# Re-placing weight preparation, weight fetches, a layer norm and down products in the feed-forward half of a transformer block

## The chip, the cores and the metric

The kernel runs on one core of a Trainium2 chip. A core has a matrix engine (TensorE, PE in the profile, with its weight loads as PEld), a vector engine (VectorE, DVE), a scalar engine (ScalarE, ACT), GpSimd (POOL) and SyncE (SP), which here only issues DMA transfers. Each engine runs its own queue of instructions in order and waits on semaphores for the others. The metric is the time of one execution in microseconds (us) on the device; lower is better.

## The reference

Input x is 2048 tokens of width 512. A conditioning vector c gives six rows of 512 (shift, scale and gate for each half). The block is an attention half and a feed-forward half, each on a layer norm:

```
h = layernorm(x) * (1 + ca) + sa
x = x + ga * attention(h)          # 32 heads, 4 segments of 512 tokens, local softmax plus a memory
h = layernorm(x) * (1 + cb) + sb
x = x + gb * (((h @ w_gate) * (h @ w_up)) @ w_down)     # hidden width 1376
```

All in float32. The change touches only the feed-forward half: layer norm, products with w_gate and w_up (512 x 1376), their elementwise product, and the product with w_down (1376 x 512) that is added to x.

## The kernel before

**Precision.** Each float32 operand is split into a high half (rounded, a copy on ScalarE) and a low half (operand minus high half, a subtraction on VectorE). A product is then three TensorE products: high x high, low x high, high x low (helper `six`, L1269, does this for two k-tiles of 128, so it issues six products).

**Feed-forward work.** The hidden width is eleven tiles f of 128 (the last, LAST = 10, is 96 wide). The four segments of 512 tokens are taken in two passes: pass p has segments 2p and 2p + 1 (index c). In a pass, pairs of tiles (i, i + 1) are computed by a scheme that gets the four blocks (two tiles x two segments) of a product with seven block products instead of eight. For this the inputs (`build`, L1223) and the weights (`wprep`, L459) are combined by additions into seven operands each, and each operand is split into halves. One such group of seven is a *unit* (`unit`, L1373): first "g" (gate), then "u" (up) for each pair. `units` (L394) is their list: n = 0 to 7 are the pairs 2, 4, 6, 8 of pass 0, n = 8 is "x" (tile LAST of pass 1, computed plainly by `open0`, `close0`, `other`), n = 9 to 18 are the pairs 2, 4, 6, 8, 0 of pass 1. Tiles 0, 1 and LAST of pass 0 are computed plainly ahead of unit 0 (L1497 to L1545).

**Inside a unit.** `unit` is a generator with six steps (its yields are numbered 1 to 6). The products go to the accumulators Z, Y, X, Y, X in turn; `out_of` copies an accumulator out on ScalarE (p5, p1, y), `add` (L1363) combines on VectorE, `finish` (L1349) multiplies gate and up (L1360) and `split` (L1289) makes the halves mH, mL of the result. The last two of the seven products, `seven` and `four`, run inside the next unit, ahead of its steps 2 and 4 (`prev(0)`, `prev(1)`). After `four` of a "u" unit, eight down products (`down`, L1323: two segments x four token tiles) go into the queue `dq`; `d()` pops one. A popped down product is 6 products into an accumulator (bank "acc"), an addition to the residual tile xa on VectorE (L1335), and for the last pair of a pass the store to the output. In pass 0 that store is followed at once by the load of the same xa buffer for pass 1 (`xload2`, L1321).

**Weights.** In pass 0, `wprep` loads raw weights, makes four sums on VectorE (tile cs), four high halves on ScalarE (cwH, L479) and four low halves on VectorE (cwL, L482). There are three buffers for prepared weights, used in turn. They are also stored to memory (`keep`). In pass 1 they are fetched back instead (`fetch`, L408: two transfers, then four copies on ScalarE, L416, in place). `wdprep` (L1297) does the same for w_down: in pass 0 load, multiply by the gate row gb (L1309), high half (L1310), low half (L1312); in pass 1 fetch and copy. `prepare(n)` joins them for unit n, as a generator of small steps.

**Order.** The Python program is unrolled by a planner that orders each engine's queue by a simulated time: an instruction that the planner believes ready may be placed ahead of instructions that stand earlier in the program. All TensorE products are chained in program order. `pin(i)` (L79) ties an instruction to the last product written before it, so that the planner cannot place it before that product; it adds no semaphore. The main loop (L1555) drives unit n, and at each step runs one step of `prepare(n + 2)` (two if unit n + 2 is a "u"), steps of other generators, and pops down products at the steps listed in `DS` (L1547):

```
DS = {"g": (1, 5, 6), "u": (1, 2, 4, 5, 6), "x": (1, 2, 4)}
if 1 <= n < CH - 1:
    next(lg, None)
```

`lg` is the layer norm of segments 2 and 3 (`lnC`, L568: loads; statistics L579, L580; scale factors; normalization L602; transposes on TensorE; L611). What of `prepare` is not done when unit n ends is run at once (`run(pr)`).

Of the kernel before, what the change touches and what calls it, by code (L numbers as in the profile page):

```python
# [8 lines left out]
F32 = mybir.dt.float32  # L9
F32R = mybir.dt.float32r  # L10
BF = mybir.dt.bfloat16
AF = mybir.ActivationFunctionType
# [6 lines left out]
S, D, H, DH, NSEG, L, F = 2048, 512, 32, 16, 4, 512, 1376  # L19
# [38 lines left out]
def tile_kernel(ctx, tc, x, wq, wk_, wv, wo, beta, w_gate, w_up, w_down, c, w_mod, out):  # L58
# [32 lines left out]
    vec, act = Switch(nc.vector), Switch(nc.scalar)  # L91
# [12 lines left out]
    btag = ["ms", "tb", "ms", "sm"]  # L104
# [49 lines left out]
    gbb = cst.tile([P, D], F32, name="gbb")  # L154
# [12 lines left out]
    def rows(s, t):  # L167
        return slice(s * L + t * P, s * L + (t + 1) * P)
# [224 lines left out]
    LAST = NF - 1  # L393
    units = [(0, nm, i) for i in range(2, LAST, 2) for nm in "gu"]  # L394
    CH = len(units)
    units += [(1, "x", LAST)] + [(1, nm, i) for i in (2, 4, 6, 8, 0) for nm in "gu"]
    NU = len(units)
    ENDS = (8, 0)
    wslot, plain = {}, {}
    wkeep, dkeep = {}, {}  # L400
# [7 lines left out]
    def fetch(key, tiles, store):  # L408
        for a, d in zip(tiles, store[key]):
            pin(nc.sync.dma_start(a.bitcast(F32), d))  # L410
        yield
        n = tiles[0].shape[1]
        for a in tiles:
            for i in range(0, n, 1024):
                b = a[:, i:min(n, i + 1024)]
                act.activation(b, b.bitcast(F32), AF.Copy)  # L416
                yield

    def xprep(n, tag, pool, rpool):
# [39 lines left out]
    def wprep(n, tag, pool, rpool):  # L459

        _, nm, i = units[n]
        if (nm, i) not in wkeep:
            raw = rpool.tile([P, KT, 2, P], F32, tag=f"raw{(n + 1) % 2}", name=f"cr{n}", bufs=1)
        wh = pool.tile([P, 7, 2, P], F32R, tag=f"wh{tag}", name=f"cwH{n}", bufs=1)
        wl = pool.tile([P, 7, 2, P], F32R, tag=f"wl{tag}", name=f"cwL{n}", bufs=1)
        wslot[n] = wh, wl
        if (nm, i) in wkeep:
            yield from fetch((nm, i), [a.rearrange("p a b c -> p (a b c)") for a in (wh, wl)], wkeep)
            return
        views = [w.rearrange("(k p) f -> p k f", p=P)[:, :, i * P:] for w in (w_gate, w_up)]  # L470
        pin(nc.sync.dma_start(raw.rearrange("p k r c -> p k (r c)"), views["gu".index(nm)][:, :, 0:2 * P]))
        yield
        S = rpool.tile([P, 4, 2, P], F32, tag="ws0", name=f"cs{n}", bufs=1)

        def A(r, c):
            return raw[:, 2 * c:2 * c + 2, r]

        def hi(d, v):
            act.activation(wh[:, d], v, AF.Copy)  # L479

        def lo(d, v):
            vec.tensor_sub(wl[:, d], v, wh[:, d].bitcast(F32))  # L482

        top = slice(4, 6), raw[:, :, 0].rearrange("p (c k) f -> p c k f", c=2)
        low = 6, A(1, 1)
        s1, s2 = ((d, S[:, d]) for d in (slice(0, 2), slice(2, 4)))
        vec.tensor_add(S[:, 0], A(1, 0), A(1, 1))
        vec.tensor_sub(S[:, 1], S[:, 0], A(0, 0))
        hi(*top)
        yield  # L490
        vec.tensor_sub(S[:, 2], A(0, 0), A(1, 0))
        vec.tensor_sub(S[:, 3], A(0, 1), S[:, 1])
        hi(*low)
        hi(*s1)
        yield
        lo(*top)
        hi(*s2)
        yield
        lo(*low)
        lo(*s1)  # L500
        yield
        lo(*s2)
        yield
# [641 lines left out]
    for v in range(-2, NQ + 1):  # L1145
        rate[0] = 5.5
        on, prev = 0 <= v < NQ, 0 <= v - 1 < NQ
        for slot in range(5):
            i = (slot + 3) % 5
            u = v + 2 if i < 3 else v + 1  # L1150
# [42 lines left out]
                    load(v + 3)  # L1193
            if slot == 1 and 3 <= v + 3 < NQ:
                until((v + 3) // 8, (v + 3) // 2 % 4)
    btag[:] = ["ms", "tb", "ms", "lk"]
    ps3 = [bank(f"wops3_{t}", shape=(P, 512)) for t in range(4)]
    for t in range(4):
        run(wo_row(ps3[t], t, us3, range(NG - 1)))
# [83 lines left out]
    def dbank(name):  # L1283
        nd[0] += 1
        return pst((P, 512), ("lq0", "lk0", "lq1", "lk1")[nd[0] % 4], name)
# [11 lines left out]
    def wdprep(p, f, tiles=None):  # L1297
        f0, n = ft[f]
        hi, lo = tiles or [bc.tile([P, D], F32R, tag="wd", name=f"d{x}{p}_{f}", bufs=8) for x in "HL"]
        wds[p, f] = hi, lo  # L1300
        if p > 0:
            yield from fetch(("d", f), (hi, lo), dkeep)
            return
        r = tmp(f"crd{p}_{f}") if tiles else wpool.tile([P, D], F32, tag="wor", name=f"crd{p}_{f}", bufs=2)
        pin(nc.sync.dma_start(r[0:n], w_down[f0:f0 + n, :]))
        if n < P:
            nc.gpsimd.memset(r[n:], 0.0)
        yield
        vec.tensor_mul(r, r, gbb)  # L1309
        act.activation(hi, r, AF.Copy)  # L1310
        yield
        vec.tensor_sub(lo, r, hi.bitcast(F32))  # L1312
        yield
        keep(("d", f), (hi, lo), dkeep)
        yield

    def xtile(p, c, t):
        x1a[p, c, t] = pc.tile([P, D], F32, tag=f"xa{c}{t}", name=f"xa{p}_{c}_{t}", bufs=1)

    def xload2(p, c, t):  # L1320
        pin(nc.sync.dma_start(x1a[p, c, t], x1d[2 * p + c][t]))  # L1321

    def down(p, fs, c, t):  # L1323
        ps = dbank(f"acc{p}_{fs[0]}_{c}_{t}")
        n = 3 * len(fs)
        j = 0
        for f in fs:
            m = ft[f][1]
            mH, mL = mids[p, f, c]
            dH, dL = wds[p, f]  # L1330
            for a, b in ((mH, dH), (mL, dH), (mH, dL)):
                pe(nc.tensor.matmul(ps, a[0:m, t * P:(t + 1) * P], b[0:m], start=j == 0, stop=j == n - 1))  # L1332
                j += 1
        xa = x1a[p, c, t]
        vec.tensor_add(xa, xa, ps)  # L1335
        if fs[0] == ENDS[p]:
            nc.sync.dma_start(out[rows(2 * p + c, t), :], xa)
            if p == 0:
                xtile(1, c, t)
                xload2(1, c, t)  # L1340

    def d(k=1):
        for _ in range(k):
            if dq:
                dq.pop(0)()
# [125 lines left out]
    def prepare(n):  # L1471

        if n >= NU:
            return
        p, nm, i = units[n]
        slot = -n % 3
        if nm == "x":
            yield from xprep(n, slot, pc, pc)
            yield from wdprep(p, LAST)
            return  # L1480
        yield from wprep(n, slot, pc, pc)
        if nm == "u":
            yield from wdprep(p, i)
            yield from wdprep(p, i + 1)
# [9 lines left out]
    pr0 = prepare(0)  # L1494
# [22 lines left out]
        next(w)  # L1517
    next(wdp[2])
    next(nb)
    next(pr0)  # L1520
    for t in range(2):
        down(0, (0, 1), 0, t)
    next(nb)
    run(close0(0, LAST))
    next(nb)
    for t in range(2, 4):
        next(pr0, None)
        down(0, (0, 1), 0, t)
    for t in range(4):
        xload2(0, 1, t)  # L1530
    run(pr0)
    pr1 = prepare(1)
    next(pr1)
    run(xp)
    for w in wdp:
        run(w)
    run(other(0, LAST))
    next(nb)
    next(nb)
    for f in (0, 1):  # L1540
        for t in (2 * f, 2 * f + 1):
            down(0, (LAST,), 0, t)
        for _ in other(0, f):
            next(pr1, None)
        next(nb)  # L1545
    dq.extend(lambda f=f, t=t: down(0, f, 1, t) for f in ((LAST,), (0, 1)) for t in range(4))
    DS = {"g": (1, 5, 6), "u": (1, 2, 4, 5, 6), "x": (1, 2, 4)}  # L1547
    lgs = []

    def lns():  # L1550
        for s in (2, 3):
            yield from lnC(s, wpool, lambda: (bc, pc)[s % 2], wpool, "orl", 4, dbank)

    lg = lns()
    for n in range(NU):  # L1555
        p, nm, i = units[n]
        pr = prepare(n + 2)
        if p == 0:
            keep((nm, i), [a.rearrange("p a b c -> p (a b c)") for a in wslot[n]], wkeep)
        if n == CH - 1:  # L1560
            nb = build(1)
        for st in (unit if nm != "x" else x_unit)(n):
            for _ in range(2 if n + 2 < NU and units[n + 2][1] == "u" else 1):
                next(pr, None)
            if n == 0:
                next(pr1, None)
                next(nb, None)
            if n == 0:
                d(1 + st % 2 if st > 1 else 1)
            elif st in DS[nm] and n < NU - 1:  # L1570
                d()
            if 1 <= n < CH - 1:
                next(lg, None)
            if n in (CH - 1, CH):
                next(nb, None)
        run(pr)
        if n == CH - 2:
            run(lg)
    tail[0]()
    d()  # L1580
    tail[1]()
# [31 lines left out]
```

## Time and profile before

| | us |
|---|---|
| median of 3 runs | 890.05 (889.26 to 891.63) |
| the profiled execution's own time | 889.4 |
| its span in the profile | 887.7 |
| TensorE busy | 849.4 (96%) |
| VectorE busy | 656.0 (74%) |
| ScalarE busy | 496.5 (56%) |
| feed-forward half, first product | 520.57 |
| unit 0, unit 8 ("x"), unit 9, unit 18: first product | 567.15, 692.26, 713.41, 846.30 |
| last down product begins | 882.26 |

The mean granted clock of TensorE over the span is 0.993 of full speed. In the profile's rows, a line number L85 or L88 is the helper for products or transposes, and L39 a helper for VectorE; tiles carry the program's names without their numbers: Xg, Xu, Yg, Yu, Zg, Zu are accumulators of gate and up, acc is a down product's, bH and bL the input halves, cwH and cwL the weight halves, dH and dL (dHp, dLp ahead of unit 0) the halves of w_down, mH and mL those of the hidden activations. "<-" in square brackets names what ended the idle time before an instruction.

### The profile page before, as it was taken

Reading aid. Unit: us, or ns where it says so; the run is one execution under the profiler, and the core shown is the slowest. Engines: PE = TensorE matmul, PEld = TensorE weight load, DVE = VectorE, ACT = ScalarE, POOL = GpSimd, SP = SyncE. Lnnn points to the kernel's source line nnn. Section 1 sums busy time; section 2 is a strip of 40 time slices with the busy share of each in tenths; the row PEclk is TensorE's granted clock in tenths of the full one; section 3 lists DMA queues with packets and bytes.
Section 4 is the critical chain, followed back from the end, with each engine's and each line's share of the span. In section 5 each row is a group of like instructions: output and inputs, shape, how many; then the busy total and the mean of one; then the engine's idle time right before and its main releaser. Section 6 shows DMA issues by size and latency. Waiting matters only on the chain.

```text
span 887.7 us, 14457 instructions
## 1 busy us (share of the span) xinstructions
PE 849.4 (96%) x4975; PEld 599.3 (68%) x4976; DVE 656.0 (74%) x1825; ACT 496.5 (56%) x755; POOL 274.8 (31%) x424
## 2 busy tenths in 40 slices
PE   8989999989999999999999998998999989999998
PEld 5755656556665556566666676876888768888876
DVE  8698777888788877788888358986977825547644
ACT  3758757677676875767545534343444725554420
POOL 4545536466555674665335500000000000000000
PEclk9999999999999999999999999999999999999999
DMA  7555334454545454466574566674643565443012
GB/s 238 148 161 144 112 113 123 150 149 140 149 100 158 140 163 106 125 200 184 167 228 137 178 204 242 222 264 152 239 184 108 213 214 209 153 177 116 16 48 95
DMA packets 83305, 141.29 MB, mean 159 GB/s; under 512 B 11712, under 2 KB 45504, under 8 KB 83232
## 3 DMA queue, kind: packets, MB, share of 16 engines
q1 hardware_dynamic: 83088, 140.35, 50.0%
q8 instruction: 39, 0.64, 0.3%
q14 instruction: 34, 0.28, 0.1%
q10 hardware_dynamic: 144, 0.02, 0.0%
HBM read 90.52 MB, written 49.55 MB: 158 GB/s over the span
## 4 chain that ended last, share of the span: by engine, by line
PE 76%; DVE 13%; ACT 6%; issue 2%; DMA 2%; POOL 1%; SPq 0%; ACTq 0%; POOLq 0%; DVEq 0%
PE acc L1332 13%; PE tb L85 8%; PE q L85 6%; PE k L85 6%; PE Xg L1274 6%; PE Xu L1274 6%; PE vps L85 5%; PE wops L85 5%; DVE q L39 4%; PE Yu L1274 4%; PE Yg L1274 4%; PE kps L85 3%; PE qps L85 3%; ACT pt L332 2%; PE Zu L1274 1%
## 5 line engine op out<-in xcount | busy, mean ns | idle before, releaser
L39 DVE CUSTOM_DVE_ANT_0 q<-q,cmask 128x384 f32<-128x384 f32 (+3 forms) x512 | 246.6, 508 | 48.9 <-PE q L85 38.7
L332 ACT ACTIVATE pt<-k 128x1024 f32<-128x1024 f32 x160 | 163.8, 1024 | 64.3 <-PE k L85 63.1
L338 POOL TENSOR_SCALAR_AFFINE_SELECT pt<-pt 128x256 f32<-128x256 f32 (+1 forms) x224 | 96.8, 446 | 166.9 <-ACT pt L332 164.5
L85 PE MATMUL q<-kst,qst 96*128 96x384 bf16 (+3 forms) x512 | 101.6, 299 | 10.9 <-DVE nm L39 9.8
L85 PE MATMUL k<-qst,kst 98*128 98x384 bf16 (+3 forms) x512 | 97.1, 302 | 5.0 <-ACT pt L332 4.9
L1335 DVE TENSOR_TENSOR xa<-xa,acc 128x512 f32<-128x512 f32 x96 | 65.7, 686 | 47.9 <-PE acc L1332 47.8
L85 PE MATMUL tb<-pt,v 128*32 128x512 f32 (+3 forms) x1024 | 75.5, 436 | 0.0
L39 DVE DVE_READ_ACCUMULATOR2_ANT nm<- 128x1 f32 x512 | 72.4, 141 | 0.0
L85 PEld LDWEIGHTS <-kst 98*128 98x128 bf16 x512 | 37.7, 98 | 49.4 <-issue 43.4
L85 PEld LDWEIGHTS <-qst 96*128 96x128 bf16 x512 | 43.2, 97 | 37.2 <-issue 13.3
L1332 PE MATMUL acc<-dH,mL 128*128 128x512 f32 (+1 forms) x152 | 60.4, 397 | 3.0 <-DVE mL L1294 3.0
L1332 PE MATMUL acc<-dH,mH 128*128 128x512 f32 (+1 forms) x152 | 60.7, 399 | 0.0
L1332 PE MATMUL acc<-dL,mH 128*128 128x512 f32 (+1 forms) x152 | 60.4, 397 | 0.0
L85 PEld LDWEIGHTS tb<-pt,v 128*32 128x32 f32 x1024 | 28.7, 109 | 38.5 <-issue 34.1
L364 ACT ACTIVATE tsb<-tb 128x512 f32<-128x512 f32 x32 | 19.0, 595 | 41.0 <-PE tb L85 41.0
L1332 PEld LDWEIGHTS acc<-dH,mL 128*128 128x128 f32 (+1 forms) x152 | 28.7, 189 | 10.2 <-DVE mL L1294 3.5
L1332 PEld LDWEIGHTS acc<-dH,mH 128*128 128x128 f32 (+1 forms) x152 | 28.7, 189 | 7.2 <-ACT mH L1293 0.4
L1332 PEld LDWEIGHTS acc<-dL,mH 128*128 128x128 f32 (+1 forms) x152 | 28.8, 189 | 7.0
L85 PE MATMUL kps<-ahH,wkH 128*128 128x512 f32 x64 | 30.1, 471 | 0.0
L1274 PE MATMUL Xu<-bH,cwH 128*128 128x512 f32 (+1 forms) x68 | 27.2, 400 | 1.8 <-DVE yu L1364 1.2
L85 PE MATMUL wops<-woH,oH 128*128 128x512 f32 x64 | 28.3, 442 | 0.7 <-ACT oH L527 0.7
L85 PE MATMUL qps<-ahH,wqH 128*128 128x512 f32 x64 | 28.7, 449 | 0.0
(378 smaller groups left out, 2040.2 us busy)
## 6 DMA issues: line engine op xcount, KB each, us to landing
wm<-in_w_mod_dram SPq DMA_DIRECT2D x24, 256.0 KB, 4.5
kd<-k SPq DMA_DIRECT2D x16, 384.0 KB, 2.5
kst<-kd SPq DMA_DIRECT2D x32, 192.0 KB, 3.2
qd<-q SPq DMA_DIRECT2D x16, 384.0 KB, 3.0
qst<-qd SPq DMA_DIRECT2D x32, 192.0 KB, 3.6
x<-in_x_dram SPq DMA_DIRECT2D x16, 256.0 KB, 4.5
kst<-kd SPq DMA_DIRECT2D x32, 128.0 KB, 3.1
qst<-qd SPq DMA_DIRECT2D x32, 128.0 KB, 3.6
```

Of the source, the lines that this page charges most:

```text
L39: i = getattr(self.eng, name)(*a, **k)
L85: return pe(nc.tensor.matmul(*a, **k))
L332: ex = act.activation(pt, kp, AF.Exp, scale=0.25)
L338: sels[u, i] = nc.gpsimd.affine_select(w, w, pattern=[[0, w.shape[1]], [1, P]], compare_op=ALU.is_ge, fill=0.0, base=0, channel_multiplier=-1)
L364: act.activation(tsbs[u], tbs.pop(u), AF.Copy)
L1274: pe(nc.tensor.matmul(ps[0:n], a, b[:, k], start=first and c == 0, stop=last and c == 5, skip_group_check=True))
L1332: pe(nc.tensor.matmul(ps, a[0:m, t * P:(t + 1) * P], b[0:m], start=j == 0, stop=j == n - 1))
L1335: vec.tensor_add(xa, xa, ps)
```

## The change

Seven edits, all in the feed-forward half:

1. `fetch`, `wprep` and the multiplication in `wdprep` get `pin`: the copies of fetched weights, the sums, the high and low halves of weights, and the scaling of w_down are tied to TensorE's place.
2. Ahead of unit 0, the steps of `pr0` (weights of unit 0) move from before and between the first down products to the block `other(0, LAST)` and the first plain block after it; the steps of `pr1` (unit 1) run beside the second plain block only, and go on in unit 0, at whose end `run(pr1)` finishes them.
3. The main loop keeps the generator of the unit before (`old`). If unit n + 2's weights are to be fetched (`wait`), the transfers are issued at step 4 of unit n and all later steps of that generator run in unit n + 1, one a step; otherwise as before.
4. `DS`: a "g" unit pops down products at steps 1 and 6 (was 1, 5, 6), a "u" unit at all six (was 1, 2, 4, 5, 6).
5. `lg` starts at unit 2 instead of unit 1.
6. One `d()` is added behind the loop, ahead of `tail[0]()`, the `seven` of the last unit.
7. The reload of xa for pass 1 is put into a list and issued two down products later (`again`, `reload`); what is left is issued ahead of the first down product of pass 1.

```diff
@@ fetch
-                act.activation(b, b.bitcast(F32), AF.Copy)
+                pin(act.activation(b, b.bitcast(F32), AF.Copy))
@@ wprep
         def hi(d, v):
-            act.activation(wh[:, d], v, AF.Copy)
+            pin(act.activation(wh[:, d], v, AF.Copy))
         def lo(d, v):
-            vec.tensor_sub(wl[:, d], v, wh[:, d].bitcast(F32))
+            pin(vec.tensor_sub(wl[:, d], v, wh[:, d].bitcast(F32)))
...
-        vec.tensor_add(S[:, 0], A(1, 0), A(1, 1))
+        pin(vec.tensor_add(S[:, 0], A(1, 0), A(1, 1)))
...
@@ wdprep
-        vec.tensor_mul(r, r, gbb)
+        pin(vec.tensor_mul(r, r, gbb))
@@ reloads
+    again = []
+    def reload():
+        c, t = again.pop(0)
+        xtile(1, c, t)
+        xload2(1, c, t)
     def down(p, fs, c, t):
+        while p == 1 and again:
+            reload()
...
             if p == 0:
-                xtile(1, c, t)
-                xload2(1, c, t)
+                again.append((c, t))
+                if len(again) > 2:
+                    reload()
@@ ahead of unit 0
-    next(pr0)
     for t in range(2):
         down(0, (0, 1), 0, t)
...
     for t in range(2, 4):
-        next(pr0, None)
         down(0, (0, 1), 0, t)
...
-    run(pr0)
     pr1 = prepare(1)
...
-    run(other(0, LAST))
+    for _ in other(0, LAST):
+        next(pr0)
...
         for _ in other(0, f):
-            next(pr1, None)
+            next(pr0, None)
+            if f == 1:
+                next(pr1, None)
         next(nb)
+    run(pr0)
...
-    DS = {"g": (1, 5, 6), "u": (1, 2, 4, 5, 6), "x": (1, 2, 4)}
+    DS = {"g": (1, 6), "u": (1, 2, 3, 4, 5, 6), "x": (1, 2, 4)}
...
@@ main loop
+    pr = iter(())
     for n in range(NU):
         p, nm, i = units[n]
-        pr = prepare(n + 2)
+        pr, old = prepare(n + 2), pr
+        wait = n + 2 < NU and units[n + 2][1:] in wkeep
...
         for st in (unit if nm != "x" else x_unit)(n):
-            for _ in range(2 if n + 2 < NU and units[n + 2][1] == "u" else 1):
-                next(pr, None)
+            next(old, None)
+            if wait:
+                if st == 4:
+                    next(pr, None)
+            else:
+                for _ in range(2 if n + 2 < NU and units[n + 2][1] == "u" else 1):
+                    next(pr, None)
...
-            if 1 <= n < CH - 1:
+            if 2 <= n < CH - 1:
                 next(lg, None)
...
-        run(pr)
+        run(old)
+        if n == 0:
+            run(pr1)
+        if not wait:
+            run(pr)
...
+    d()
     tail[0]()
     d()
     tail[1]()
```

More of the change, by code (lines that the diff above doesn't have):

```diff
@@ L486, in wprep @@
         s1, s2 = ((d, S[:, d]) for d in (slice(0, 2), slice(2, 4)))
-        vec.tensor_add(S[:, 0], A(1, 0), A(1, 1))
-        vec.tensor_sub(S[:, 1], S[:, 0], A(0, 0))
+        pin(vec.tensor_add(S[:, 0], A(1, 0), A(1, 1)))
+        pin(vec.tensor_sub(S[:, 1], S[:, 0], A(0, 0)))
         hi(*top)
         yield
-        vec.tensor_sub(S[:, 2], A(0, 0), A(1, 0))
-        vec.tensor_sub(S[:, 3], A(0, 1), S[:, 1])
+        pin(vec.tensor_sub(S[:, 2], A(0, 0), A(1, 0)))
+        pin(vec.tensor_sub(S[:, 3], A(0, 1), S[:, 1]))
         hi(*low)
@@ L1195, in tile_kernel @@
                 until((v + 3) // 8, (v + 3) // 2 % 4)
-    btag[:] = ["ms", "tb", "ms", "lk"]
+    btag[:] = ["lk", "ms", "ms", "tb"]
     ps3 = [bank(f"wops3_{t}", shape=(P, 512)) for t in range(4)]
@@ L1308, in wdprep @@
         yield
-        vec.tensor_mul(r, r, gbb)
+        pin(vec.tensor_mul(r, r, gbb))
         act.activation(hi, r, AF.Copy)
         yield
-        vec.tensor_sub(lo, r, hi.bitcast(F32))
+        pin(vec.tensor_sub(lo, r, hi.bitcast(F32)))
         yield
```

## The prediction

> **What bounds the kernel now.** I read the page first, then who TensorE waits for, then stretches of 10 us, then the instructions around each wait. The page gives the span and the busy times:
>
> ```profile
> span 887.7 us, 14457 instructions
> PE 849.4 (96%) x4975; PEld 599.3 (68%) x4976; DVE 656.0 (74%) x1825; ACT 496.5 (56%) x755; POOL 274.8 (31%) x424
> ```
>
> TensorE (PE) is busy for 96%, so only its remaining waits can be won by an edit that removes no product. The diff touches the feed-forward half alone, from about 520 us on. There the list of what TensorE waited for (us in total, times, longest) is short:
>
> ```profile
> PE acc L1332 <- DVE mL L1294: 3.7, 2, 3.0
> PE Yg L1274 <- ACT p5g L1384: 3.2, 1, 3.2
> PE acc L1332 <- ACT mH L1293: 2.0, 1, 2.0
> PE Xu L1274 <- DVE yu L1364: 1.2, 2, 0.9
> PE Xg L1274 <- DVE xr L39: 0.8, 1, 0.8
> PE Xu L1274 <- DVE p5u L1364: 0.6, 1, 0.6
> ```
>
> That is 11.5 us, of which the 0.8 for xr lies ahead of everything changed. The timeline of TensorE (start, duration, line, operation, idle before it) places the three large ones:
>
> ```profile
> 536.34 0.40 PE L1332 MATMUL acc<-dHp,mL 128*128 128x512 f32 x1
> 536.57 0.39 PE L1332 MATMUL acc<-dLp,mH 128*128 128x512 f32 x1
> 538.93 0.49 PE L1332 MATMUL acc<-dHp,mH 128*128 128x512 f32 x1 [1.97 <-ACT mH L1293]
> 540.15 0.50 PE L1332 MATMUL acc<-dHp,mL 128*128 128x512 f32 x1 [0.72 <-DVE mL L1294]
> ...
> 602.63 0.50 PE L1332 MATMUL acc<-dH,mH 128*128 128x512 f32 x1
> 606.08 0.59 PE L1332 MATMUL acc<-dH,mL 128*128 128x512 f32 x1 [2.95 <-DVE mL L1294]
> 610.07 0.39 PE L1332 MATMUL acc<-dH,mH 128*128 128x512 f32 x1
> 611.00 0.40 PE L1332 MATMUL acc<-dH,mL 128*128 128x512 f32 x1
> 613.31 0.39 PE L1332 MATMUL acc<-dH,mH 128*128 128x512 f32 x1
> ...
> 718.77 0.39 PE L1274 MATMUL Xg<-bL,cwH 128*128 128x512 f32 x1
> 722.35 0.77 PE L1274 MATMUL Yg<-bH,cwH 128*128 128x512 f32 x1 [3.19 <-ACT p5g L1384]
> 725.88 0.40 PE L1332 MATMUL acc<-dL,mH 128*128 128x512 f32 x1
> ```
>
> The usual distance from product to product is 0.23 us (first two rows), so a block of six takes 1.4. A loss is start to start less 0.23. **Stall A**: (2.36 - 0.23) + (1.22 - 0.23) = 3.1 us. **Stall D**: 3.45 - 0.23 = 3.2; then two products, four transposes and six products take 3.99 us (606.08 to 610.07), where the same sequence takes 2.31 (611.00 to 613.31): another 1.7, so 4.9. **Stall E**: 3.58 - 0.23 = 3.35; then eight steps take 3.53 us where 8 x 0.23 is 1.84: another 1.7, so 5.0. After idle times of 2.95 and 3.19 us the products run slowly for a while; after 1.97 they don't. The short ones, by the list: B and C (yu 0.3, p5u 0.6, at 594 and 599 us) and F (yu 0.9, at 857 us) are 1.8. All that can be won is 3.1 + 4.9 + 5.0 + 1.8 = 14.8 us.
>
> **The change, part by part.** The sum is made against the profiled execution, 889.4 us; the median of the runs, 890.05, is 0.65 above it, and 0.3% (2.7 us) is about what tells a change from none here.
>
> *Weight preparation before unit 0 moved behind the first down products, and tied.* VectorE's rows at stall A, and the two groups of low halves:
>
> ```profile
> 537.60 0.69 DVE L482 TENSOR_TENSOR cwL<-cs,cwH 128x512 fp32r<-128x512 f32 x1
> 538.81 0.68 DVE L482 TENSOR_TENSOR cwL<-cs,cwH 128x512 fp32r<-128x512 f32 x1
> 539.41 0.69 DVE L1294 TENSOR_TENSOR mL<-gs,mH 128x512 fp32r<-128x512 f32 x1
> ...
> L482 DVE TENSOR_TENSOR cwL<-cs,cwH 128x512 fp32r<-128x512 f32 x20 | 13.2, 684 | 0.0
> L482 DVE TENSOR_TENSOR cwL<-cr,cwH 128x512 fp32r<-128x512 f32 (+1 forms) x20 | 10.4, 552 | 0.4 <-ACT cwH L479 0.4
> ```
>
> The late mL stands behind two low halves of unit 0's weights, which are needed 30 us later. A unit's four low halves are 2 x 0.68 + 2 x 0.55 = 2.5 us, and its four sums of half that width (bounded by 4 x 0.55) 2.2 at most: up to 4.7 us of VectorE, and four high halves of ScalarE, leave the stretch before 540; the load of the raw weights stays where it is. A tie adds no wait on the chip: it forbids the planner a place earlier in the engine's queue than what stands behind TensorE's last product in the program. GpSimd has no part in any of this (0.00 busy in the rows below). Against the removal, the multiplication of w_down by the gate (0.69 by the nearest row, the one of mL, equal in shape) is now tied to TensorE's last product: two of them, and the high and low halves that follow, now fall between the end of close0(0, 1) at 533 us and the down product at 536. That is 2 x 0.69 + 2 x 0.69 = 2.8 us of VectorE in 3 us. So A keeps something: between all (3.1, or worse by 2.8) and nothing. I take 2.0 won, nearer to the removal, since 4.7 leaves for 2.8 that comes.
>
> *The third segment's norm one unit later, down products one block later, unit 1's preparation spread into unit 0.* VectorE in stretches of 10 us (columns: stretch, sum, then busy us and instructions of PE, PEld, DVE, ACT, POOL; clock; DMA) and at D:
>
> ```profile
> 570.00:580.00 10.00, 10.00 (x45) 8.21 (x44) 7.81 (x14) 2.57 (x5) 0.00 (x0) 1.00 0.64 211
> 580.00:590.00 10.00, 10.00 (x45) 8.18 (x44) 8.66 (x19) 3.76 (x8) 0.00 (x0) 1.00 0.50 174
> 590.00:600.00 10.00, 9.01 (x39) 6.75 (x38) 10.00 (x25) 6.24 (x14) 0.00 (x0) 1.00 1.00 382
> 600.00:610.00 10.00, 7.05 (x25) 5.21 (x24) 7.83 (x16) 4.28 (x8) 0.00 (x0) 0.83 0.55 197
> ...
> 583.09 0.69 DVE L579 BATCH_NORM_STATS2 cst<-x 128x6 f32<-128x512 f32 x1
> 602.91 1.92 DVE L602 TENSOR_SCALAR x<-x,cmv,cy 128x512 f32<-128x512 f32 x4
> 605.34 0.69 DVE L1294 TENSOR_TENSOR mL<-p5g,mH 128x512 fp32r<-128x512 f32 x1
> ```
>
> VectorE runs without a gap from 590 on, and the mL that TensorE waits for at D stands right behind the four normalizations. Moving the norm (its four loads on SyncE move along, a step ahead of their use as before) takes 4 x 0.69 = 2.8 us out of unit 1 (from 582) and 1.9 out of unit 2 (from 592); the four statistics come back into unit 2, ahead of the mL at worst: relief at D between 1.9 and 4.7 us. The rest of unit 1's w_down (two steps of 0.69) falls from before unit 0 into the end of unit 0: 1.4 back. Popping the first down product at step 6 instead of step 5 gives a block, 1.4 us. Less B and C, which bring TensorE 0.9 earlier, the slack is between 1.9 - 1.4 + 1.4 - 0.9 = 1.0 and 3.8, against 3.2 needed: D's wait falls to between 2.2 and nothing, and with it the slow stretch. I take 1.2 left: D wins 3.7. B and C go with the statistics: 0.8 of 0.9.
>
> *Fetches a unit ahead.* What ScalarE and SyncE do at E, and two sizes:
>
> ```profile
> 713.08 0.37 SPq L410 DMA_DIRECT2D cwL<-keptLg  x1
> 720.03 1.79 ACT L416 ACTIVATE cwL<-cwL 128x1024 fp32r<-128x1024 f32 x2 [5.72 <-DMA cwL<-keptLg]
> 721.72 0.58 ACT L1384 ACTIVATE p5g<-Yg 128x512 f32<-128x512 f32 x1
> ...
> cwH<-keptHg SPq DMA_DIRECT2D x4, 896.0 KB, 6.4
> ACT dH L416 <- DMA dH<-keptHd: 21.8, 7, 8.7
> ```
>
> The copies of unit 11's weights stood in ScalarE's queue ahead of p5g, and their data took 7 us to come. After the change the transfer of unit n+2 is issued at step 4 of unit n and its copies are placed in unit n+1, behind that unit's earlier work, so p5g in unit 9 has ahead of it only copies whose transfer began a unit before. From step 4 to step 1 of the next unit lie four blocks (1.4 each, 5.6 us) against 6.4 for landing, so ScalarE may stand for about 1 us where nothing is due yet: E wins between 3.3 (its wait without the slow stretch) and 5.0; I take 4.7. SyncE issues nothing new and gets the w_down fetches after the next unit's weights; they wait there for a free buffer, with nothing urgent behind.
>
> [...]
>
> *Reloads behind, and one down product ahead of the last unit's tail.* Each xa reload on SyncE waited for the store of the same buffer:
>
> ```profile
> SPq L1321 <- DMA out_dram<-xa: 22.9, 8, 6.7
> ```
>
> No wait of TensorE names xa, so this wins 0, hidden under VectorE's slack; if a reload came late, its add would hold VectorE, not TensorE, which has four accumulator banks. The extra down product fills 1.4 us where F was 0.9: all of it goes. The number of products is the same.
>
> *New waits.* Unit 0's 4.7 us of preparation goes into 547 to 567, unit 1's into unit 0, where VectorE has 2.2 us free (the row of 570). Between none and 2.5 us (4.7 - 2.2); I take 1.0, as part of it is off any path.
>
> Sum: 2.0 + 0.8 + 3.7 + 4.7 + 0.9 - 1.0 = 11.1 us; 889.4 - 11.1 = **878.3**.
>
> **The rivals.** (1) Only the second pass gains: the moves in the first pass shift VectorE's load without lowering it, and A to D stay in size elsewhere. For it: VectorE is full from 590 on and the work is the same. Against: 570 to 590 has 3.5 us free. E and F: 889.4 - 5.6 = 883.8. (2) It does not do what it says: the ties order the program, they add no wait on the chip, and the queues come out as before; F and little else go, 888.5. Against: counts of steps moved too. (3) Slower: fetched copies late for their own unit. Nine units' copies now run in the unit before use, the fourth placed at step 4, three blocks (4.2 us) ahead of the first product that needs it. Two held transfers ahead of it, at the mean of the list for dH, 21.8 / 7 = 3.1 us each, exceed that by 2.0; nine times is 18 us: 878.3 + 18 = 896. It decides from 11.1 / 9 = 1.2 us per unit. For it: a hold of 8.7 us occurred. Against: none but E has cost TensorE anything. [...]
>
> **How the numbers follow.** The forecast 0.61 (own range 873.5 to 882), rival 1 0.18, rival 2 0.06, rival 3 0.15. All 14.8 won is 874.6, and about 1 us beyond since short waits lose more than their idle time; so 873.5 below. Above, 887 leaves out rival 3 and most of rival 2. Faster: 0.61 + 0.18 + 0.01 = 0.80; same 0.05 (rival 2); slower 0.15.
>
> **What would show it.** Right: no idle over 2.5 us on TensorE after 540, no stretch with clock 0.83, p5g ahead of copies with landed data, xr still 0.8. Wrong: waits for cwL or cwH at the start of units after 713 (rival 3); a wait for mL near 575 or 602 as long as before (rival 1); dHp the last to come at 536 (A worse).

## The result, and the profile after

The median after is 880.05 us (four runs, 877.95 to 881.08) against 890.67 for the kernel before on the same chip: ratio 0.9879, 95% interval 0.9855 to 0.9902. The profiled execution took 879.9 us; 878.3 had been forecast. The page's span and busy times, and the list of what TensorE waited for in the second half (total, times, longest):

```profile
span 878.2 us, 14439 instructions
PE 845.7 (96%) x4976; PEld 596.4 (68%) x4976; DVE 655.6 (75%) x1825; ACT 496.6 (57%) x755; POOL 274.4 (31%) x424
```

```profile
PE Xu L1274 <- DVE yu L1374: 1.7, 2, 1.3
PE Xu L1274 <- DVE p5u L1374: 1.5, 1, 1.5
PE acc L1341 <- DVE mL L1294: 1.5, 2, 1.3
...
PE acc L1341 <- ACT mH L1293: 0.5, 1, 0.5
```

(The diff moves lines down by about ten: L1341 is the down product that was L1332, L1374 the addition that was L1364, L1394 the copy that was L1384.) VectorE, ScalarE and GpSimd are as busy as before; TensorE is 3.7 us less busy, about as much as the two slow stretches behind D and E took (1.7 each). The waits went from 11.5 us to 5.2. None is for p5g or xr any more, and none is longer than 1.5. The timeline of TensorE after, with its waits in order of time:

```profile
517.00 0.49 PE L85 MATMUL wops<-woH,oH 128*128 128x512 f32 x1 [0.69 <-ACT oH L527]
...
536.27 0.39 PE L1341 MATMUL acc<-dLp,mH 128*128 128x512 f32 x1
537.16 0.51 PE L1341 MATMUL acc<-dHp,mH 128*128 128x512 f32 x1 [0.51 <-ACT mH L1293]
537.89 0.51 PE L1341 MATMUL acc<-dHp,mL 128*128 128x512 f32 x1 [0.22 <-DVE mL L1294]
...
592.50 0.50 PE L1274 MATMUL Xu<-bH,cwH 128*128 128x512 f32 x1 [1.28 <-DVE yu L1374]
...
601.70 0.40 PE L1341 MATMUL acc<-dH,mH 128*128 128x512 f32 x1
603.36 0.50 PE L1341 MATMUL acc<-dH,mL 128*128 128x512 f32 x1 [1.26 <-DVE mL L1294]
...
735.39 0.50 PE L1274 MATMUL Xu<-bH,cwH 128*128 128x512 f32 x1 [0.45 <-DVE yu L1374]
...
741.30 0.50 PE L1274 MATMUL Xu<-bH,cwH 128*128 128x512 f32 x1 [1.49 <-DVE p5u L1374]
...
873.90 0.40 PE L1341 MATMUL acc<-dL,mH 128*128 128x512 f32 x1
```

A loss is again start to start less 0.23, so some 0.15 to 0.3 more than the idle time in brackets. A (537) costs 1.16 instead of 3.1, D (603) 1.43 instead of 4.9, and E and F are not there. B (592) has grown from 0.54 to 1.44. New are two waits in unit 11, at 735 and 741 us, 0.60 + 1.65 = 2.25. And no stretch of the second half has a low clock now. VectorE in the stretches of the prediction's table, with the clock third from the right:

```profile
590.00:600.00 10.00, 8.72 (x38) 6.64 (x37) 10.00 (x22) 5.23 (x11) 0.00 (x0) 1.00 1.04 403
600.00:610.00 10.00, 8.74 (x39) 6.79 (x38) 9.11 (x23) 2.78 (x7) 0.00 (x0) 1.00 0.89 317
```

TensorE gained 1.7 us between 600 and 610 (8.74 busy against 7.05), with VectorE still full from 590 to 600 and busier than before behind that (9.11 against 7.83).

To compare kernels without the attention half, in which executions of the same code differ by up to 2.6 us here, I use the distance from the product that waits for oH (517.00 above) to the last down product's last row (873.90): the *second half*. Before, the two rows are

```profile
516.27 0.49 PE L85 MATMUL wops<-woH,oH 128*128 128x512 f32 x1 [0.69 <-ACT oH L527]
...
883.43 0.40 PE L1332 MATMUL acc<-dL,mH 128*128 128x512 f32 x1
```

367.16 us before, 356.90 after: 10.3 won. The spans differ by 9.5, as the row at oH stands 0.7 later after the change.

### The profile page after: what moved, and what is told of

Same layout as the page of the kernel before. It is cut to its first block, busy times and chain, and to the rows that moved or that the text cites. A ratio compares the mean times of both kernels' runs of the same rounds, so it can differ in the third digit from the quotient of the medians.

```text
span 878.2 us, 14439 instructions
## 1 busy us (share of the span) xinstructions
PE 845.7 (96%) x4976; PEld 596.4 (68%) x4976; DVE 655.6 (75%) x1825; ACT 496.6 (57%) x755; POOL 274.4 (31%) x424
## 4 chain that ended last, share of the span: by engine, by line
PE 75%; DVE 12%; ACT 6%; DMA 4%; issue 2%; POOL 1%; SPq 0%; ACTq 0%; POOLq 0%; DVEq 0%
PE acc L1341 14%; PE tb L85 8%; PE q L85 6%; PE k L85 6%; PE Xu L1274 5%; PE Xg L1274 5%; DVE q L39 5%; PE wops L85 5%; PE vps L85 4%; PE Yu L1274 4%; PE Yg L1274 4%; PE kps L85 3%; PE qps L85 3%; ACT pt L332 2%; PE Zu L1274 1%
## 5 line engine op out<-in xcount | busy, mean ns | idle before, releaser
L1341 PE MATMUL acc<-dH,mL 128*128 128x512 f32 (+1 forms) x152 | 60.0, 395 | 1.3 <-DVE mL L1294 1.3
L1341 PE MATMUL acc<-dH,mH 128*128 128x512 f32 (+1 forms) x152 | 60.3, 397 | 0.0
L1341 PE MATMUL acc<-dL,mH 128*128 128x512 f32 (+1 forms) x152 | 60.1, 395 | 0.0
L1341 PEld LDWEIGHTS acc<-dH,mL 128*128 128x128 f32 (+1 forms) x152 | 28.5, 188 | 8.4 <-DVE mL L1294 1.7
L1341 PEld LDWEIGHTS acc<-dL,mH 128*128 128x128 f32 (+1 forms) x152 | 28.6, 188 | 7.0
L1341 PEld LDWEIGHTS acc<-dH,mH 128*128 128x128 f32 (+1 forms) x152 | 28.5, 188 | 6.8
```

## The experiments

Every kernel in one table; "second half" is read from its own profile in the way shown above. Ratios are to the kernel before, measured on the same chip each time (its medians there are 890.2 to 891.1). A second half is one execution, and one slow stretch more or less is worth some 1.7 us of it.

| kernel | median us | ratio, 95% interval | second half |
|---|---|---|---|
| before | 890.67 | | 367.16 |
| changed | 880.05 | 0.9879 (0.9855 to 0.9902) | 356.90 |
| no_ties | 884.55 | 0.9932 (0.9911 to 0.9954) | 361.55 |
| prep0_early | 879.72 | 0.9874 (0.9854 to 0.9894) | 356.04 |
| norm_early | 882.92 | 0.9921 (0.9898 to 0.9943) | 359.99 |
| fetch_in_unit | 883.38 | 0.9911 (0.9879 to 0.9942) | 362.31 |
| ds_old | 881.22 | 0.9902 (0.9875 to 0.9929) | 360.50 |
| reload_now | 880.20 | 0.9886 (0.9857 to 0.9914) | 359.00 |
| bank_last | 890.61 | 1.0000 (0.9986 to 1.0013) | 369.44 |
| ties_only | 887.86 | 0.9972 (0.9959 to 0.9986) | 363.73 |
| lag4 | 877.80 | 0.9856 (0.9840 to 0.9872) | 354.52 |
| norm3 | 878.16 | 0.9861 (0.9846 to 0.9876) | 356.03 |
| norm3_lag4 | 877.62 | 0.9855 (0.9834 to 0.9875) | 353.31 |
| spread | 876.03 | 0.9834 (0.9812 to 0.9855) | 351.83 |

By the intervals of the medians only no_ties, ties_only and bank_last stand clear of the changed kernel, and spread just touches it. What is said below of the other runs rests on the waits in their traces.

### The ties: without them, and alone

no_ties is the changed kernel with the nine new ties off, ties_only the kernel before with them on (one of the nine, on the low halves of w_down, is not named in the list of edits above):

```diff
-            pin(act.activation(wh[:, d], v, AF.Copy))
+            act.activation(wh[:, d], v, AF.Copy)
...
-        pin(vec.tensor_mul(r, r, gbb))
+        vec.tensor_mul(r, r, gbb)
```

> All moves of the change kept, the nine new ties taken off. If the moves alone do it (my theory: each part acts where it was moved), the four large stalls stay cured: TensorE waits at 537 us for mH and mL no longer than 1.2 us in all, at 602 for mL no longer than 2 us, no stretch at a low clock, and the time is that of the changed kernel within 1.5 us (878.5 to 881.5). If the ties do the work (rival), the weight preparation goes back ahead of mL: stall A returns with about 3.1 us idle and stall D with over 2.5 us, and the time is 884 or more.

Measured 884.55, 4.5 us above the changed kernel. The stall is at A again, and at the same TensorE product as before the change: the fourth of the first down product, which waits for the second mH. The timeline of no_ties, ScalarE and TensorE:

```profile
532.43 0.94 ACT L479 ACTIVATE cwH<-cr 128x512 fp32r<-128x512 f32 x2 [1.68 <-DMA cr<-in_w_gate_dram]
...
538.49 0.64 ACT L479 ACTIVATE cwH<-cs 128x512 fp32r<-128x512 f32 x1
...
540.01 0.63 ACT L479 ACTIVATE cwH<-cs 128x512 fp32r<-128x512 f32 x1
...
541.00 0.63 ACT L1293 ACTIVATE mH<-gs 128x512 fp32r<-128x512 f32 x1
...
541.69 0.79 PE L1341 MATMUL acc<-dHp,mH 128*128 128x512 f32 x1 [3.09 <-ACT mH L1293]
```

Unit 0's high halves (cwH), written behind these down products in the program, stand ahead of the last mH in ScalarE's queue: the planner drew them forward. The same instructions of the kernel before, with the VectorE row that makes mH's input:

```profile
529.67 0.94 ACT L479 ACTIVATE cwH<-cr 128x512 fp32r<-128x512 f32 x2 [0.74 <-DMA cr<-in_w_gate_dram]
...
535.80 0.68 DVE L1360 TENSOR_TENSOR gs<-gs,Xu 128x512 f32<-128x512 f32 x1
...
538.24 0.64 ACT L1293 ACTIVATE mH<-gs 128x512 fp32r<-128x512 f32 x1
```

In both kernels ScalarE's order between the first and the last of these rows is the same, ScalarE works there without a gap, and mH starts 8.57 us behind the first row. That row waits until unit 0's raw weights have landed. So the move by itself changed nothing in ScalarE's queue here, and my theory for this run fell at A. These rows also show what A's longer wait was: mH's input was there at 536.5, and mH started 1.8 us later; ahead of it in ScalarE's queue stood, among other work, four high halves, the first of which had waited for its load. At D the waits stayed as in the changed kernel (1.0 for mL), and E stayed away: those do not hang on the ties.

> The kernel before with the nine new ties alone, nothing moved. My theory, after the run without ties (they keep the planner from placing moved work 5 us early, but move nothing themselves): the waits at 537 for mH and mL shorten from 3.1 to about 1.6, as unit 0's low halves can no longer stand ahead of mL; D at 603 and E at 722 stay with their slow stretches: 887.5 to 889.5, ratio 0.997 to 0.999. Rival 2 of the prediction (a tie adds no wait and changes nothing): 890, ratio 1.000. Second rival (the ties do most of the work): D or E goes too, 885 or less.

Measured 887.86, ratio 0.9972: as expected, A alone shortens (1.13 + 0.49 = 1.62 us). D and E stay, E with 2.67 us idle. The second half is 3.4 shorter, of which 1.5 is A and most of the rest a slow stretch that did not come at D this time (last section). A tie does change the order that comes out, so rival 2 is wrong even for the ties alone; but what they carry is 1.5 to 3 of the 10 us.

### Unit 0's preparation back at its old place

```diff
+    next(pr0)
     for t in range(2):
         down(0, (0, 1), 0, t)
...
     for t in range(2, 4):
+        next(pr0, None)
         down(0, (0, 1), 0, t)
...
+    run(pr0)
     pr1 = prepare(1)
...
-    for _ in other(0, LAST):
-        next(pr0)
+    run(other(0, LAST))
```

> Unit 0's weight preparation put back ahead of and between the first four down products, all else as in the changed kernel, ties included. My theory (stall A came from the low halves in VectorE's queue ahead of mL): two low halves of 0.68 us and two shorter ones come back there, A's idle time is 3.1 us again against 1.2 in the changed kernel, and the time rises by 1.5 to 2.5 us, 881.5 to 882.5. Rival (the late mL and mH at 537 come from the w_down multiplications and ScalarE, whatever stands there): A stays at 1.2 us, 880.

Measured 879.72: the time is the rival's, and my theory fell. A costs 1.13 + 0.49 = 1.62 us against 1.16, so the move is worth half a microsecond at most; with the ties only the first sums and one high half can stand ahead of mH. (In this run unit 11 lost 0.98 us instead of 2.25, which hides that half.) A's gain of 2.0 is the ties' 1.5 and the move's 0.5; without the ties the move leaves the order as it was.

### The third segment's norm: back in unit 1, and on to unit 3

```diff
-            if 2 <= n < CH - 1:
+            if 1 <= n < CH - 1:
```

> The third segment's norm back in unit 1, all else as in the changed kernel. My theory (D was the four normalizations ahead of the last mL of units 1 and 2): the wait for mL near 602 grows from 1.4 to 2.5 or more, with a slow stretch if it passes about 2.9; the time rises by 1.5 to 5 us, 881.5 to 885. Rival (the popping of the down products one block later is what cured D): D stays under 1.5 us and the time within 1 us of the changed kernel's 880.

Measured 882.92, 2.9 more. D is back and takes another form: the transposes of the norm themselves wait for the normalization. TensorE's timeline:

```profile
597.90 0.39 PE L1274 MATMUL Yg<-bL,cwH 128*128 128x512 f32 x1
601.69 0.85 PE L88 MATMUL ctp<-ident,x 128*128 128x128 f32 x2 [3.40 <-DVE x L602]
```

3.79 - 0.23 = 3.6 us, with a slow stretch of products 0.43 apart behind it. B is down to 0.17, and unit 11 had no wait in this run, so the net is smaller than D's return; by the medians it is at the edge of the noise. Moved the other way (`3 <= n`):

> The third segment's norm another unit later, in unit 3. My theory (the waits at 592 for yu and 603 for mL, 1.4 us each, are VectorE's queue, full from 586 to 605 with the four statistics in it): the one at 603 goes, as four statistics (2.7 us) leave unit 2, the one at 592 stays, since its add stands behind low halves and w_down multiplications alone; a new short wait may come in unit 3 or 4: 878.3 to 880. Rival (the wait moves along with the norm, as it did from unit 1 to unit 2): as much or more in unit 3 or 4 and at the start of the second pass, 880 to 883.

Measured 878.16. The wait at 603 is gone and the one at 592 stays at 1.44; a new one of 0.47 comes at 627. That is the theory in all three points (the time is 0.1 below its range). Unit 11's waits (0.49 + 1.80) are untouched.

### The old places of the down products

```diff
-    DS = {"g": (1, 6), "u": (1, 2, 3, 4, 5, 6), "x": (1, 2, 4)}
+    DS = {"g": (1, 5, 6), "u": (1, 2, 4, 5, 6), "x": (1, 2, 4)}
```

> The down products popped at the steps they had before (1, 5, 6 and 1, 2, 4, 5, 6), the last extra one kept, all else as in the changed kernel. My theory: the one at 603 comes a block of six products (1.4 us) earlier, and its wait for mL grows from 1.4 to 2.8 us, near the idle time that brings the slow stretch: 881.4, or 883 with the stretch. Rival (the first product of a pair waits for mH and mL of its own unit only, which comes late in every unit or none): no change over 0.5 us, 880.

Measured 881.22 (interval to 0.9929, so little above the noise by the medians), and 3.6 us more in the second half of the profiled execution, which was the longest of its four (879.92 to 884.97). The wait for mL at 604 is 1.76 us instead of 1.26, not the 2.8 expected, and a wait for p5u of 1.80 comes at 734. Both are followed by a slow stretch:

```profile
604.25 0.50 PE L1341 MATMUL acc<-dH,mL 128*128 128x512 f32 x1 [1.76 <-DVE mL L1294]
...
734.25 0.51 PE L1274 MATMUL Yu<-bH,cwH 128*128 128x512 f32 x1 [1.80 <-ACT p5u L1394]
```

```profile
605.00:610.00 5.00, 5.00 (x16) 3.95 (x16) 3.08 (x8) 0.51 (x2) 0.00 (x0) 0.67 1.01 337
...
735.00:740.00 5.00, 5.00 (x17) 3.97 (x16) 3.42 (x6) 1.40 (x3) 0.00 (x0) 0.70 0.97 378
```

So the later popping gives D 0.5 us of idle time, not the 1.4 of the block that I counted, and here the slow stretch on top. At 734 p5u stood in ScalarE's queue behind three copies of fetched weights, the first at 731.83. That is the pattern shown below for unit 11; whether it has the same cause was not tested.

### The fetches back in their own unit

```diff
-            next(old, None)
-            if wait:
-                if st == 4:
-                    next(pr, None)
-            else:
-                for _ in range(2 if ... else 1):
-                    next(pr, None)
+            for _ in range(2 if ... else 1):
+                next(pr, None)
```

> The fetches of the second pass back in the unit that they were in before, ties and reload lag kept. My theory (E is the copies in ScalarE's queue that wait for their transfer ahead of p5g): E returns at the start of unit 9 with about 3 us idle and the slow stretch behind it, 5.0 us, and the two waits of unit 11 (0.6 and 1.7) either go or stay: 882.7 to 885. Rival (the ties alone, which put the copies behind TensorE's place, are enough): no idle over 1.5 us at the start of unit 9, and 878 to 880.5.

Measured 883.38, 3.3 more, 5.4 in the second half. What TensorE waited for there names E:

```profile
PE Yg L1274 <- ACT p5g L1394: 2.5, 1, 2.5
PE Xg L1274 <- ACT p1g L1394: 1.5, 1, 1.5
```

ScalarE's rows in this run:

```profile
713.83 1.06 ACT L416 ACTIVATE cwL<-cwL 128x1024 fp32r<-128x1024 f32 x1 [5.80 <-DMA cwL<-keptLg]
714.79 0.58 ACT L1394 ACTIVATE p5g<-Yg 128x512 f32<-128x512 f32 x1
```

The copy that waits for its transfer stands ahead of p5g again, ties or not, and a slow stretch follows (clock 0.69 from 720 to 725 us). So the fetch a unit ahead is what cures E. Unit 11's waits shrink to 0.60; that the fetch a unit ahead makes them is not shown by it, as they were also small in runs that keep it (0.98 in prep0_early, none in norm_early).

### Reloads: no lag, and a longer one

Where unit 11's waits come from is read from the queues after the change: SyncE, ScalarE and VectorE between 709 and 742 us, in the timeline.

```profile
709.98 0.38 SPq L410 DMA_DIRECT2D cwH<-keptHg  x1
710.46 0.38 SPq L410 DMA_DIRECT2D cwL<-keptLg  x1
711.37 0.34 SPq L1346 DMA_DIRECT2D out_dram<-xa  x1
...
721.16 1.63 SPq L1321 DMA_DIRECT2D xa<-x1d  x2
722.88 0.38 SPq L1346 DMA_DIRECT2D out_dram<-xa  x1
726.14 0.32 SPq L1321 DMA_DIRECT2D xa<-x1d  x1
726.55 0.38 SPq L410 DMA_DIRECT2D dH<-keptHd  x1
...
732.44 0.32 SPq L1321 DMA_DIRECT2D xa<-x1d  x1
732.87 0.37 SPq L410 DMA_DIRECT2D cwH<-keptHu  x1
...
737.60 1.79 ACT L416 ACTIVATE cwH<-cwH 128x1024 fp32r<-128x1024 f32 x2 [3.70 <-DMA cwH<-keptHu]
739.30 0.61 ACT L1293 ACTIVATE mH<-yg 128x512 fp32r<-128x512 f32 x1
...
739.95 0.69 DVE L1294 TENSOR_TENSOR mL<-yg,mH 128x512 fp32r<-128x512 f32 x1 [2.82 <-ACT mH L1293]
740.56 0.68 DVE L1374 TENSOR_TENSOR p5u<-Xu,p5u 128x512 f32<-128x512 f32 x1
```

Read it backwards. TensorE waited at 741.30 for p5u; that stood behind mL in VectorE's queue, mL behind mH, mH in ScalarE's queue behind copies whose transfer had been issued only at 732.87. In SyncE's queue reloads of xa stood ahead of that transfer, each waiting until the store of its buffer had landed (11.9 us in five waits between 700 and 745 us, in the list below). The store of 711.37 was issued right behind 1.8 MB of weights, and its reload went out 9.8 us later; of the transfers that touch xa in this stretch, stores and reloads, the trace says

```profile
DMA to landing us min/median/max: 2.0/3.1/9.9
```

This store landed 9.8 us after its issue, at 721.2, and the reload of another buffer issued right behind it (711.80) after 9.9, at 721.7, against 2.0 at best; the second half of the fetch, issued at 710.46, had landed after 10.0 us, at 720.5. That the small store stood behind the large fetch is my reading of these times; the trace does not show the order in which the queue was worked off. Two runs test the chain, one without any lag (`len(again) > 0`), and one with a longer lag, the last four reloads one by one and the two segments of the last tile's down products in the other order. The second run's edit:

```diff
-        while p == 1 and again:
+        if p == 1 and again:
             reload()
...
-                if len(again) > 2:
+                if len(again) > 4:
                     reload()
...
-        dq.extend(lambda c=c, t=t: down(1, (LAST,), c, t) for c in (0, 1) for t in range(4))
+        dq.extend(lambda c=c, t=t: down(1, (LAST,), c, t) for c in (1, 0) for t in range(4))
```

> The changed kernel with each reload issued four stores behind its own store instead of two, the last four one per down product instead of together. My theory (unit 11's two waits, 0.6 and 1.7 us, come from SyncE standing behind a store of xa that lands only after the 1.8 MB of weights fetched ahead of it, so that w_down and unit 12's weights are issued late): the issue of unit 12's cwH comes at least 3 us earlier relative to the start of unit 11, ScalarE's waits of 4.5 and 3.7 us shrink, and 1.5 to 2.3 us of TensorE's waiting goes: 877.7 to 878.6. Rival (the copies stand ahead of mH in ScalarE's queue, late or not): the two waits stay over 1.5 us in all, 880.

Measured 877.80, and 354.52 in the second half, 2.4 less: unit 11 has no wait at all. The three parts of the edit are not separated. SyncE's waits between 700 and 745 us, changed kernel and then lag4:

```profile
SPq L1321 <- DMA out_dram<-xa: 11.9, 5, 4.5
```

```profile
SPq L1321 <- DMA out_dram<-xa: 3.0, 1, 3.0
```

Unit 12's cwH is issued 3.2 us ahead of unit 11's start (730.78 against 733.94) instead of 0.2 behind it. ScalarE's wait for the w_down copy falls from 4.51 to 1.16 us. It still waits 3.27 us for cwH, though, which costs TensorE nothing: what counted was how late the data came, not that ScalarE waited.

> The changed kernel with the reload lag taken off: each reload is issued right behind its own store, as before the change. The prediction counted the lag at nothing, hidden. After the longer lag won 2.25 us, my theory is that without any lag SyncE stands longer at each reload, so that w_down and unit 12's weights come later still: the waits in unit 11 grow from 2.25 us to 3 or more, 881 to 884. Rival (the lag of two is as good as none, since only the last four reloads hold SyncE): within 0.7 us of 880.05.

Measured 880.20, median equal to the changed kernel's: the rival by the medians. In its profiled execution (883.06, the longest of four, 878.35 to 883.06) unit 11's wait is 2.35 us at once, with a slow stretch behind it (clock 0.73 from 745 to 750 us), as the theory has it. The queues speak for the rival: in the changed kernel, too, the last two reloads (726.14 and 732.44 above) stand directly behind the stores of their own buffers (722.88 and 727.50, landed 3.2 and 4.9 us later), just as without the lag (stores at 722.92 and 727.84, reloads at 726.52 and 733.13). So the lag of two did not reach the place where it would have counted, and the 2.1 us that this execution's second half lost are not shown to be the lag's. The longer lag with its two companions is worth 2.3 by the medians, whose intervals overlap, and 2.4 by the second half. (Where nothing of the reloads was changed, unit 11 lost 2.25, 2.29, 1.2, 1.0, 0.6 or nothing: presumably it depends on when TensorE comes there against the transfers.)

### The bank order, and the last down product

One line of the diff is not among the seven edits listed above, and the prediction left it out: the order in which the last attention segment's sums take the accumulator banks. This run has it and edit 6 alone, on the kernel before.

```diff
-    btag[:] = ["ms", "tb", "ms", "lk"]
+    btag[:] = ["lk", "ms", "ms", "tb"]
...
+    d()
     tail[0]()
```

> The kernel before with two far-apart edits of the change alone: the banks of the last attention segment in the changed order, and one down product ahead of the last unit's tail. My theory: the wait for yu at 857 us (0.9 us) goes with the down product; the wait for xr at 520 (0.8 us), which went although I expected it to stay, goes with the bank order: the time is 1.7 us under that of before, ratio 0.998. Rival (the wait for xr went through some other edit): it stays at 0.8 us, and the ratio is 0.999.

The waits for xr (0.94 at 520) and for yu at 857 (1.01) are both gone from its timeline, each at its own place. The ratio is 1.000 all the same: with the old order of preparation, A grew from 3.1 to 5.4 us of losses, at 541 one of 3.05 for mH with a slow stretch (clock 0.70 from 540 to 545 us). The rows at A explain it: the high halves of unit 0's raw weights now wait 2.61 us for their load and begin at 532.31, and the last mH starts 8.57 us behind them, as in the kernel before and in no_ties. The load itself was issued 2.4 us later than before (525.44 against 523.04); why is open. With the ties at most one of those high halves stands ahead of mH, and with the preparation at its old place A is 1.62 us with either bank order (ties_only, prep0_early). So in these runs the bank order pays only with the ties.

### Putting it together

> The changed kernel with the norm in unit 3 and the longer reload lag together. My theory (the two act in different places and add): the waits at 603 (1.4 us) and in unit 11 (2.25 us) are both gone, of the second half's waits only those at 537 (1.2), 592 (1.4) and 627 (0.5) are left: 880.05 - 1.4 + 0.5 - 2.25 = 876.9. Rival (shorter waits ahead bring TensorE into the next one sooner): one of them comes back and the time is that of the better of the two alone, 877.8 to 878.2.

The waits come out as the theory says: neither at 603 nor in unit 11 any, 0.53 at 628, and a second half of 353.31, 3.6 below the changed kernel. The median, 877.62, can't be told from that of lag4 alone, as the rival had it: that the two add is shown by the waits, not by the time.

```diff
-                for _ in range(2 if n + 2 < NU and units[n + 2][1] == "u" else 1):
-                    next(pr, None)
+                next(pr, None)
...
-        if not wait:
-            run(pr)
```

> The same with the preparation of an up unit of the first pass taken one step at a time, and what is left of it carried into the next unit instead of run at the end of its own. My theory (the add for yu at 592 stands in VectorE's queue behind two w_down multiplications, 1.3 us, and low halves tied into the end of unit 1): those multiplications come in unit 2, the wait of 1.4 us falls under 0.5, and the time is about 1 us under the same kernel without it, 875.9. Rival (the low halves alone hold the add, or unit 2 now gets them ahead of its own mL): the wait stays or comes at 596 to 603, 877.

Measured 876.03, ratio 0.9834: with the longer lag and the later norm this is 4.0 us below the changed kernel, the fastest here (the intervals just touch, at 0.9855). Against the same kernel without the spreading (877.62) the medians do not decide; the waits do. What TensorE still waits for in its second half:

```profile
PE acc L1341 <- ACT mH L1293: 0.5, 1, 0.5
PE Xu L1274 <- DVE yu L1374: 0.4, 1, 0.4
...
PE acc L1341 <- DVE mL L1294: 0.2, 1, 0.2
```

B fell from 1.44 to 0.53 as its add no longer stands behind two w_down multiplications: those two were most of B's 1.44, and not the statistics.

## Why the prediction was right, step by step

The sum was 11.1 us, the second half gave 10.3, and the profiled executions differ by 9.5. The mechanisms of D, E and F were right; A, B, C and the new waits came out for other reasons than those given. That the sum still came within 1 us is in part luck, as errors of its terms cancelled.

- **A, 2.0 of 3.1 taken: 1.96 measured.** The size was right, the reason half. I read A as low halves ahead of mL on VectorE, and gave the gain to the removal of 4.7 us of VectorE. That fits the shorter of its two losses (0.99); the longer one (2.13) was mH, behind high halves in ScalarE's queue that began only when their weights had landed. The runs show that the ties alone win 1.5 and the move 0.5; without ties, the planner draws the same work forward again, and the kernel is 4.5 slower than with them. I had written that a tie "forbids the planner a place earlier" and then costed the move as if the place in the program settled it.
- **B and C, 0.8 of 0.9: minus 0.1 measured.** They were 0.54 and 0.76, and one wait of 1.44 took their place. The step "B and C go with the statistics" failed: norm3 takes the four statistics out of unit 2 and the wait stays; spread takes the two multiplications away and it falls to 0.53.
- **D, 3.7 of 4.9: 3.5 measured**, with a wait of 1.26 left where 1.2 was taken. The norm carries it (norm_early brings back 3.6 and the slow stretch); the popped block gave 0.5 of idle time where I had 1.4.
- **E, 4.7 of 5.0: all 5.0.** ScalarE's copies in front of p5g were the cause, as fetch_in_unit shows.
- **F, 0.9:** gone, as counted.
- **New waits, 1.0 between 547 and 567 and in unit 0: 2.25 in unit 11.** None came between 547 and 567 or in unit 0. The place was wrong by the step on SyncE, "nothing urgent behind": behind the waiting reloads stood w_down and unit 12's weights. The premise is rival 3's (copies in ScalarE's queue held by late transfers), in one unit instead of nine: SyncE stands behind stores only while the reloads run. The outcome is not rival 3's: TensorE never waited for the fetched weights themselves, but for p5u and yu, which stood behind the held copies.
- **The reloads, 0:** true of the lag of two, which left the last reloads directly behind their stores; not of reloads as such, as the longer lag won 2.3.
- **xr "still 0.8": gone.** The edit that took it, the bank order, was in the diff and not priced. Its 0.94 and E's 0.3 made up for more than half of what the new waits took beyond their term (1.25) and B and C did not give (0.9). This is the luck in the sum.

By places: 1.96 - 0.14 + 3.5 + 5.05 + 1.01 - 2.25 + 0.94 = 10.1, against 10.3 in the second half.

Rival 1 fell, as the first pass gained 5.3 us; rival 2 fell by ties_only; of rival 3 the held copies came true in one unit, the slower time did not.

## What to carry to other kernels

Where a planner orders each engine's queue, a move in the program can be worth nothing until something ties it there (A, and the reloads with the lag of two), while other moves hold without a tie (D and E): look at the queue that comes out, not at the place in the source. Before calling a queue's wait harmless, list what stands behind it: here transfers for the next unit stood behind reloads, which waited for stores, one of which landed only 9.8 us after its issue, right after a large fetch. And once the long waits are cut, look at bursts: here one step of preparation at a time instead of two took a wait from 1.44 to 0.53, where moving other work away from it (norm3) had left it.

## What the runs showed of the hardware that I had not expected

In these runs the length of an idle time alone did not decide whether the products behind it ran slowly. The prediction read from the trace before that 2.95 and 3.19 us bring the slow stretch and 1.97 does not. In ds_old, 1.76 and 1.80 us did (clocks 0.67 and 0.70, in the rows above). In ties_only, 2.95 us at D, the same wait as before the change, did not:

```profile
606.28 0.50 PE L1332 MATMUL acc<-dH,mL 128*128 128x512 f32 x1 [2.95 <-DVE mL L1294]
```

```profile
605.00:610.00 5.00, 3.72 (x18) 3.08 (x19) 3.72 (x7) 0.78 (x1) 0.00 (x0) 1.00 0.65 238
```

In the other traces waits of 2.35 (reload_now, clock 0.73 from 745 to 750 us), 2.67 (ties_only, at E, 0.66 from 720 to 725) and 3.09 us (no_ties, 0.51 from 540 to 545) brought the slow stretch too, and none of 1.64 us or less did by itself (1.64 in norm3, clock 1.00 from 738 to 744). So in these runs a wait between 1.76 and 2.95 us went either way, and a slow stretch cost about 1.7 us or more (no_ties ran its products 0.43 apart from 542 to 547). What decides it is not shown, as no run varied the length or the place of a wait alone; nor is it shown whether a part of the spread between executions of one kernel is this.
